# Decay attention and a two-layer hard-swish network on one core: the second layer's scale in another PSUM bank, its float32 pieces two places further ahead, and the last tile's units in another order

## The chip, the cores and the metric

One core of a Trainium2 chip runs the whole program. The metric is the device time of one execution in microseconds. Besides the median of several timed runs there is one profiled execution, whose trace gives every instruction's start and duration; times "at 139" are microseconds from the start of its span.

## The reference

The input is 8 batches of 8 heads, 576 positions and 64 numbers a head; the first layer has 512 by 2048 weights, the second 2048 by 512. The weights arrive as float64, two 32-bit words each, so they have to be decoded on the chip.

```python
scores = scale * q @ k.T + (cum[:, None] - cum[None, :])   # cum: cumulative sum of log f
scores = where(causal, -1e9, scores)
attn   = softmax(scores)                                   # per head, 576 x 576
x      = (attn @ v)                                        # heads side by side: 4608 x 512
h      = x @ w_in                                          # 4608 x 2048
g      = h * clip(h + 3, 0, 6) / 6
out    = g @ w_out                                         # 4608 x 512
```

## The kernel before, in words

**Engines.** TensorE (PE) multiplies, VectorE (DVE) and ScalarE (ACT) evict PSUM and do the elementwise work, GpSimd (POOL) prepares q and k, SyncE (SP) issues the DMAs. Each engine takes its instructions in one fixed order, which a scheduler makes at build time from program order, priorities and its own model of durations. So a change of a buffer can move hundreds of instructions.

**Two halves that run beside each other.** The attention goes head by head. The first batch is done in another form (four pairs, then eight heads, tiles `pf` and `ps`); from the second batch on each head ("F" in `VH`, 56 of them) goes through `rows`: PE makes scores `pn` (L609, L612) in two halves, DVE takes row maxima while copying to `pp` (L620), ACT takes the exponential (L632) and a float16 copy (L646), DVE or POOL the remainder (L649, L655), a transposing DMA moves both (L667), PE multiplies with v into `pav` (L692 to L697), and DVE normalises it. Every two heads a transposing DMA (`x_move`, L748) puts the result into `xT`, the input of the network.

**The network** works on tiles of 512 tokens, one per batch. For each of 16 pieces of 128 hidden features `h_unit` does 12 matmuls (L775 to L777; every number is split into two float16 halves, and three of the four products are summed), then ACT L781, DVE L784, ACT L785, DVE L786 write the two halves of `gT`. Then `out_unit` makes 128 rows of output with 48 matmuls of 512 columns (L821 to L823, tile `po`), ACT L827 scales them and SP stores them (L830). Each batch has 64 tokens more than its tile; the left-over tokens of two batches make one short unit (`h_short`, L797 to L799, tile `phs`, evicted by L805, L809, L811, L812). `queue` and `fill` hand these units out between the steps of the attention. The first tile's units are named by their columns, 0 or 256, since its first 256 columns are ready earlier.

**PSUM.** The network's accumulators rotate over three banks: two of pool `ps_m` (tag `mm`) and the single bank of `ps_t` (tag `tr`), which the small transposes of the row maxima (`ptm`, L500) use too.

**The second layer's weights.** `w_out_work` loads 16 chunks, decodes each to float32 and squares it (L251 to L257), then sums the squares over all chunks (L279) and lets `pow2_scale` (L184 to L196, tile `pt_w`) make one power of two out of it. With that scale `w_split` makes two float16 halves of each chunk: the high one on ACT (L284), the low one on DVE (L295). Both float32 piece and halves live in one buffer, `w2`: the halves of chunk k in place k, the float32 piece of chunk k in place k+1. So the high half of chunk k is written over the float32 piece of chunk k-1, and ACT must wait until DVE has read that one.

**The last tile** (`moe_tile` with t = 7) runs its 16 `h_unit`s, then the four `h_short`s of the last two batches (their `gT` lies in `vst`), then four `out_unit`s of 512 columns and two of 256 columns for the short rows.

Of the kernel before, what the change touches and what calls it, by code (L numbers as in the profile page):

```python
# [20 lines left out]
def kernel(  # L21
# [10 lines left out]
    nc = tc.nc  # L32
# [68 lines left out]
    NSP = 3  # L101
# [32 lines left out]
    w2 = cpool.tile([P, NFC + 1, 2, DM], F16, name="w2")  # L134
# [46 lines left out]
    def pow2_scale(pm, s_col, i_col, name):  # L181
        pool, tag = (ps_t, "tr") if SV < s_col < SV + B else (ps_m, "mm")
# [37 lines left out]
    slots_in = slots_out + [spare[:, (2 * h + 9) * CW:(2 * h + 11) * CW] for h in range(NSP)]  # L220

    def w_chunk(i, k):

        if i == 0:
            j, c = divmod(k, NCC)
            cols = slice(j * CW, (j + 1) * CW)
            o = (2 * j + c % 2 + NW // 2 * (c // 2)) * CW
            return w_in[c * P:(c + 1) * P, cols], gTf[:, o:o + CW], [t[:, c, cols] for t in w1]
        return (
            w_out[k * P:(k + 1) * P, :], w2f[:, (k + 1) * CW:(k + 2) * CW],  # L230
            [w2[:, k, h, :] for h in range(2)],
        )
# [526 lines left out]
    turn = [0]  # L759

# [7 lines left out]
    def h_unit(t, fc, c0, c1):  # L768
        x = xT[t % 2]
# [3 lines left out]
        for cc in range(NCC):  # L773
            xh, xl = (x[:, cc, c0 // P:c1 // P, hl] for hl in range(2))
            nc.tensor.matmul(ph, w1[0][:, cc, fs_], xh, start=(cc == 0), stop=False)  # L775
            nc.tensor.matmul(ph, w1[0][:, cc, fs_], xl, start=False, stop=False)  # L776
            nc.tensor.matmul(ph, w1[1][:, cc, fs_], xh, start=False, stop=(cc == NCC - 1))  # L777
            if cc == 1 and nw == TT:
                yield H_COST
        r = p2.tile([P, TT], F32, tag="rt", name=f"r_{t}_{fc}_{c0}", bufs=3)[:, :nw]  # L780
# [8 lines left out]
    def h_short(u, j, gd):  # L789
# [3 lines left out]
        for i in range(n):  # L793
            fs_ = slice((n * j + i) * P, (n * j + i + 1) * P)
            for cc in range(NCC):
                xh, xl = (x[:, cc, :, hl] for hl in range(2))
                nc.tensor.matmul(ph[:, i], w1[0][:, cc, fs_], xh, start=(cc == 0), stop=False)  # L797
                nc.tensor.matmul(ph[:, i], w1[0][:, cc, fs_], xl, start=False, stop=False)
                nc.tensor.matmul(ph[:, i], w1[1][:, cc, fs_], xh, start=False, stop=(cc == NCC - 1))  # L799
            if i == 1:  # L800
                yield H_COST
        r = p2.tile([P, TT], F32, tag="rt", name=f"rs_{u}_{j}", bufs=3)
# [30 lines left out]
    def moe_tile(t, c0=0, c1=TT):  # L833
        for fc in range(NFC):
# [5 lines left out]
            yield from h_unit(t, fc, c0, c1)  # L840
        if t == 0:
# [4 lines left out]
        last = t == B - 1  # L846
        if last:
            gs = vst.bitcast(F16).rearrange("p c e -> p (c e)")[:, 0:2 * NFC * P]
            gs = gs.rearrange("p (a f t) -> p a f t", a=2, f=NFC)
            for j in range(NG):  # L850
                yield from h_short(t // 2, j, gs)
# [223 lines left out]
```

## Time and profile before

| | |
|---|---|
| median of 3 runs | 1078.44 us (1075.19 to 1080.29) |
| the profiled execution | 1080.35 us, of which the span is 1078.6 us |
| mean granted TensorE clock | 0.985 |
| busy share of the span | PE 94%, DVE 67%, ACT 55%, POOL 38% |

The page divides the span into 40 slices of 27 us. The stages by the trace: the first batch's attention and the decoding of the weights to 137 us, the first heads of the second batch and the first tile's two layers to 255 us, then seven batches in an even rhythm to 925 us, and the last tile alone to the end. "Idle before, releaser" in a row says how long the engine sat before the instruction and what ended it. A matmul's shown duration includes its way through the array, so the distance of two starts, not the duration, is its price: 512 columns start about 0.216 us apart.

### The profile page before, as it was taken

The page shows a single profiled execution, that of the slowest core. Times are in us where ns is not written, and L with a number is a line of the kernel's source. Part 1 is how long each engine was busy: PE and PEld are TensorE (multiplying, and loading weights), DVE is VectorE, ACT ScalarE, POOL GpSimd, SP SyncE. Part 2 cuts the span into 40 slices and gives each one's busy share as a digit, 9 for nine tenths or more (in the row PEclk, how much of TensorE's full clock was granted, in tenths as well). Part 3 has the DMA queues.
Part 4 walks back from the last instruction along what each step waited for, and adds up shares of the span by engine and source line. Part 5 has one row for each costly group of instructions (what it writes and reads, how often), then busy time and mean ns, then how long its engine had stood idle before and what let it go on. Part 6 is the DMA issues. An engine that isn't in the chain of part 4 may idle for free.

```text
span 1078.6 us, 21257 instructions
## 1 busy us (share of the span) xinstructions
PE 1013.8 (94%) x7698; PEld 604.8 (56%) x7698; DVE 726.8 (67%) x1903; ACT 587.9 (55%) x1190; POOL 408.5 (38%) x505
## 2 busy tenths in 40 slices
PE   2799988899999999999999999999999999999897
PEld 2557854665455755555555755555555755544545
DVE  7887899887875668866865677767855678305300
ACT  4777657665664557555654547655743567315301
POOL 7434456454433445443434334443433442000000
PEclk9989989999999999999999999999999999999999
DMA  8976448965665676567465576567565554300000
GB/s 253 288 210 199 117 103 160 203 149 127 149 104 121 138 151 128 111 151 160 98 127 107 105 164 129 118 137 169 101 112 123 108 101 84 78 30 1 1 20 30
DMA packets 259300, 133.79 MB, mean 124 GB/s; under 512 B 226964, under 2 KB 228812, under 8 KB 259196
## 3 DMA queue, kind: packets, MB, share of 16 engines
q1 hardware_dynamic: 259196, 132.44, 55.7%
q8 instruction: 61, 1.00, 0.4%
q14 instruction: 43, 0.35, 0.1%
HBM read 47.93 MB, written 9.73 MB: 53 GB/s over the span
## 4 chain that ended last, share of the span: by engine, by line
PE 66%; DVE 13%; DMA 6%; ACT 6%; issue 5%; POOL 2%; SPq 1%; ACTq 0%; DVEq 0%; POOLq 0%
PE po L821 10%; PE po L822 10%; PE po L823 10%; PE ph L775 7%; PE ph L776 7%; PE ph L777 7%; DVE pp L620 3%; PE pn L609 3%; PE pn L612 3%; DMA vst<-in_vS_dram 2%; ACT pp L632 2%; DVE ring L649 2%; DVE gT L786 1%; DVE r L784 1%; DMA ring<-in_w_out_dram 1%
## 5 line engine op out<-in xcount | busy, mean ns | idle before, releaser
L632 ACT ACTIVATE pp<-pp,nb 128x192 f32<-128x192 f32 x280 | 138.9, 552 | 135.8 <-DVE nb L626 135.3
L821 PE MATMUL po<-w,gT 128*128 128x512 f16 x560 | 208.0, 383 | 5.2 <-DVE rs L809 2.8
L822 PE MATMUL po<-w,gT 128*128 128x512 f16 x560 | 210.2, 383 | 1.3 <-DVE w L295 1.3
L775 PE MATMUL ph<-xT,w 128*128 128x512 f16 (+1 forms) x576 | 201.5, 359 | 10.3 <-DVE r L784 10.1
L823 PE MATMUL po<-w,gT 128*128 128x512 f16 x560 | 210.1, 382 | 0.0
L776 PE MATMUL ph<-xT,w 128*128 128x512 f16 (+1 forms) x576 | 200.7, 358 | 0.0
L777 PE MATMUL ph<-xT,w 128*128 128x512 f16 (+1 forms) x576 | 200.0, 358 | 0.0
L649 DVE TENSOR_TENSOR ring<-pp,ring 128x128 f16<-128x128 f32 (+2 forms) x216 | 140.4, 660 | 82.6 <-ACT ring L646 81.6
L620 DVE CUSTOM_DVE_ANT_0 pp<-pn,W 128x192 f32<-128x192 f32 x280 | 123.3, 482 | 26.6 <-PE pn L612 25.0
L447 POOL TENSOR_SCALAR TK<-ST 64x576 fp32r<-64x576 f32 (+1 forms) x68 | 49.9, 733 | 240.8 <-PE pn L609 200.7
L459 POOL TENSOR_TENSOR T<-ST,T 64x576 fp32r<-64x576 f32 (+1 forms) x68 | 99.4, 1461 | 84.2 <-DMA T<-TK 72.5
L609 PE MATMUL pn<-TK,TQ 68*128 68x192 f32 x336 | 124.3, 384 | 5.0 <-issue 3.9
L784 DVE SCALAR_TENSOR_TENSOR r<-r,ph 128x512 f32<-128x512 f32 (+1 forms) x144 | 89.1, 620 | 56.2 <-ACT r L781 55.8
L785 ACT CAST gT<-r 128x512 f16<-128x512 f32 (+1 forms) x144 | 81.5, 568 | 80.8 <-DVE r L784 80.2
L786 DVE TENSOR_TENSOR gT<-r,gT 128x512 f16<-128x512 f32 (+1 forms) x144 | 103.9, 725 | 20.6 <-ACT gT L785 19.0
L781 ACT ACTIVATE r<-ph,bias_r,SC 128x512 f32<-128x512 f32 (+1 forms) x144 | 103.9, 725 | 23.1 <-PE ph L777 20.6
L646 ACT CAST ring<-pp 128x192 f16<-128x192 f32 x280 | 114.3, 449 | 0.0
L612 PE MATMUL pn<-T,T 128*128 128x192 f32 x336 | 113.0, 363 | 0.0
L456 POOL TENSOR_TENSOR T<-ST,TQ 64x576 fp32r<-64x576 f32 (+2 forms) x68 | 98.3, 1446 | 15.9 <-PE ps L552 5.4
L823 PEld LDWEIGHTS <-gT 128*128 128x128 f16 x560 | 55.0, 99 | 68.3 <-issue 9.2
L655 POOL TENSOR_TENSOR ring<-pp,ring 128x128 f16<-128x128 f32 x96 | 61.6, 642 | 80.5 <-ACT ring L646 35.2
L822 PEld LDWEIGHTS <-gT 128*128 128x128 f16 x560 | 54.9, 99 | 63.5 <-issue 8.5
(154 smaller groups left out, 1987.1 us busy)
## 6 DMA issues: line engine op xcount, KB each, us to landing
ST<-in_qk_dram SPq DMA_DIRECT2D x64, 288.0 KB
T<-TK SPq DMA_DIRECT2D x64, 144.0 KB
out_dram<-o SPq DMA_DIRECT2D x33, 256.0 KB
ring<-in_w_out_dram SPq DMA_DIRECT2D x16, 512.0 KB
T<-TQ SPq DMA_DIRECT2D x56, 144.0 KB
vst<-in_vS_dram SPq DMA_DIRECT2D x7, 1040.0 KB
ring<-in_w_in_dram SPq DMA_DIRECT2D x9, 512.0 KB
w<-in_w_in_dram SPq DMA_DIRECT2D x7, 512.0 KB
```

The costliest lines, as they stand in the source:

```text
L609: nc.tensor.matmul(dst, TQ[i][0:D + 4, qs], TK[i][0:D + 4, a:e], start=True, stop=False)
L612: nc.tensor.matmul(dst, T7[j][:, qs], T1[j][:, a:e], start=False, stop=True)
L620: nc.vector.tensor_tensor_reduce(pp[:r, w:w + kw], pn[:r, o:o + kw], W[:r, 4 * P + r - kw:4 * P + r], 1.0, -3.0e38, ALU.add, ALU.max, accu ...
L632: nc.scalar.activation(x_, x_, AF.Exp, bias=nb[:r, e0 + x:e0 + x + 1], scale=0.125)
L649: eng.tensor_tensor(hl[:r, a:a + c * P], pp[:r, at[c] + 64:at[c] + kw], hl[:r, h0[c] + 64:h0[c] + kw], op=ALU.subtract,)
L775: nc.tensor.matmul(ph, w1[0][:, cc, fs_], xh, start=(cc == 0), stop=False)
L776: nc.tensor.matmul(ph, w1[0][:, cc, fs_], xl, start=False, stop=False)
L777: nc.tensor.matmul(ph, w1[1][:, cc, fs_], xh, start=False, stop=(cc == NCC - 1))
L786: nc.vector.tensor_tensor(gT[:, 1, fc, c0:c1], r, gT[:, 0, fc, c0:c1], op=ALU.subtract)
L821: nc.tensor.matmul(po, g[:, 0, fc, ts_], w2[:, fc, 0, c], start=(fc == 0), stop=False)
L822: nc.tensor.matmul(po, g[:, 0, fc, ts_], w2[:, fc, 1, c], start=False, stop=False)
L823: nc.tensor.matmul(po, g[:, 1, fc, ts_], w2[:, fc, 0, c], start=False, stop=(fc == NFC - 1))
```

## The change

It has three parts. The sum matrix `pt_w` of the second layer's power of two is allocated in the single bank of `ps_t` in place of one of the two `mm` banks. The float32 pieces lie three places ahead of their halves (`AHEAD = 3`), so `w2` has 19 places for 17; three spare slots for the first layer's raw loads move with it. And in the last tile each `h_short` comes after every fourth `h_unit`, with each unit's first matmul of a column chunk ordered behind the last matmul of the unit before (an order for the scheduler; both are on PE).

```diff
-    NSP = 3
...
-    w2 = cpool.tile([P, NFC + 1, 2, DM], F16, name="w2")
+    AHEAD = 3
+    w2 = cpool.tile([P, NFC + AHEAD, 2, DM], F16, name="w2")
...
-        pool, tag = (ps_t, "tr") if SV < s_col < SV + B else (ps_m, "mm")
+        pool, tag = (ps_t, "tr") if SV < s_col < SV + B or s_col == S2 else (ps_m, "mm")
...
-    slots_in = slots_out + [spare[:, (2 * h + 9) * CW:(2 * h + 11) * CW] for h in range(NSP)]
+    slots_in = slots_out + [spare[:, o * CW:(o + 2) * CW] for o in (13, 15, 17)]
...
-            w_out[k * P:(k + 1) * P, :], w2f[:, (k + 1) * CW:(k + 2) * CW],
+            w_out[k * P:(k + 1) * P, :], w2f[:, (k + AHEAD) * CW:(k + AHEAD + 1) * CW],
...
+    chain = []
+
+    def behind(on):
+        return tc.issue_after(chain[-1]) if on and chain else nullcontext()
...
     def h_unit(t, fc, c0, c1):
+        last = t == B - 1
...
-            nc.tensor.matmul(ph, w1[0][:, cc, fs_], xh, start=(cc == 0), stop=False)
+            with behind(last and cc == 0):
+                nc.tensor.matmul(ph, w1[0][:, cc, fs_], xh, start=(cc == 0), stop=False)
...
+        if last:
+            chain.append(d.ins)
...
     def h_short(u, j, gd):
...
+                with behind(gd is not gT and cc == 0):
+                    nc.tensor.matmul(ph[:, i], w1[0][:, cc, fs_], xh, start=(cc == 0), stop=False)
...
+        if gd is not gT:
+            chain.append(d.ins)
...
     def moe_tile(t, c0=0, c1=TT):
...
             yield from h_unit(t, fc, c0, c1)
+            if last and new == 1:
+                yield from h_short(t // 2, j, gs)
...
-            for j in range(NG):
-                yield from h_short(t // 2, j, gs)
```

In the listings below, a line number of the changed program is higher than the old one: L295 stays, L775 is L781, L786 is L794, L799 is L808, L821 to L823 are L834 to L836, L827 is L840.

**DVE, ahead of the first head of the second batch.** Row maxima of that head are the L620 rows on `pn_12`. Before, these rows stand there; `SC` is the table of scales, `rs`, `xf` and `pav` belong to the first batch's attention, and `w2<-w2` is a low half of a second-layer chunk.

```order
L724 RECIPROCAL rs_10_0_1642<-rs_10_0_1642 128x3
L384 TENSOR_TENSOR SC_121<-SC_121 128x1
L726 TENSOR_SCALAR rs_10_0_1642<-rs_10_0_1642,SC_121 128x3
L620 ISA pp_12_0_1670,MF0_108<-pn_12_0_1661,W_88 128x192
L620 ISA MF0_108 128x1
L620 ISA pp_12_0_1670,MF0_108<-pn_12_0_1661,W_88 128x576
L620 ISA MF0_108 128x1
L620 ISA pp_12_0_1670,MF0_108<-pn_12_0_1661,W_88 64x64
L620 ISA MF0_108 64x1
L387 COPY SC_121<-SC_121 64x1
L727 TENSOR_TENSOR xf_10_1640<-pav_110,rs_10_0_1642 128x3x64
L295 SCALAR_TENSOR_TENSOR w2_115<-w2_115,SC_121 128x512
```

In the changed program these rows lead up to the same L620 (`r` and `gT` are evictions of the first tile's features, `vm1` a maximum over v).

```order
L295 SCALAR_TENSOR_TENSOR w2_115<-w2_115,SC_121 128x512 x3
L792 SCALAR_TENSOR_TENSOR r_0_13_0_1168<-r_0_13_0_1168,ph_0_13_0_1155 128x256
L794 TENSOR_TENSOR gT_116<-r_0_12_0_1142,gT_116 128x256
L366 TENSOR_REDUCE vm1_1579<-vst_112 128x1 x2
L721 TENSOR_SCALAR rs_9_1_1550<-pav_110 128x3
L295 SCALAR_TENSOR_TENSOR w2_115<-w2_115,SC_121 128x512 x3
L794 TENSOR_TENSOR gT_116<-r_0_13_0_1168,gT_116 128x256
L371 TENSOR_TENSOR vm1_1579<-vm1_1579 128x2
L792 SCALAR_TENSOR_TENSOR r_0_14_0_1204<-r_0_14_0_1204,ph_0_14_0_1191 128x256
L724 RECIPROCAL rs_9_1_1550<-rs_9_1_1550 128x3
L792 SCALAR_TENSOR_TENSOR r_0_15_0_1232<-r_0_15_0_1232,ph_0_15_0_1219 128x256
L620 ISA pp_12_0_1670,MF0_108<-pn_12_0_1661,W_88 128x192
```

Before, the first low half stands behind the first head's first row maxima and the others are strewn over the following heads. Now nine of the 16 (one and two more stand further up) are ahead of it, and the other seven follow before the second head.

**PE, at the second head of the second batch.** The second head's scores are `pn_13`; `po_0` and `po_128` are the first two output units of the first tile. Before, the second head's scores stand behind the first matmul of each.

```order
L777 LDWEIGHTS w11_114
L777 MATMUL ph_0_2_256_1905<-xT0_117,w11_114 128x256
L821 LDWEIGHTS gT_116
L821 MATMUL po_0_0_1389<-w2_115,gT_116 128x512
L821 LDWEIGHTS gT_116
L821 MATMUL po_128_0_1525<-w2_115,gT_116 128x512
L609 MATMUL pn_13_0_1744<-TK1_97,TQ1_94 128x192
L612 MATMUL pn_13_0_1744<-T11_100,T71_102 128x192
```

In the changed program all 96 matmuls of these two units stand ahead of it; their last three and the head's first two are these.

```order
L834 LDWEIGHTS gT_116
L834 MATMUL po_128_0_1525<-w2_115,gT_116 128x512
L835 LDWEIGHTS gT_116
L835 MATMUL po_128_0_1525<-w2_115,gT_116 128x512
L836 LDWEIGHTS gT_116
L836 MATMUL po_128_0_1525<-w2_115,gT_116 128x512
L609 MATMUL pn_13_0_1744<-TK1_97,TQ1_94 128x192
L612 MATMUL pn_13_0_1744<-T11_100,T71_102 128x192
```

So the second head has moved behind 94 matmuls of 512 columns. The third to eighth heads follow behind it, with the rest of the first tile's features between them, and 27 matmuls of the second tile now stand ahead of the third batch's third head (`pn_22`), where before the first of them stood behind it.

**ACT, at the end of the program.** `po_4480` is the last 512-column output unit, `po_3456_0` and `po_3456_256` are the two units of the short rows. The last rows before are these.

```order
L827 ACTIVATE o_4352_0_12420<-po_4352_0_12371,SC_121 128x512
L827 ACTIVATE o_4480_0_12472<-po_4480_0_12423,SC_121 128x512
L805 ACTIVATE rs_3_3_12261<-phs_3_3_12212,bias_r_86,SC_121 128x4x64 x2
L811 CAST vst_112<-rs_3_3_12261 128x512
L827 ACTIVATE o_3456_0_12524<-po_3456_0_12475,SC_121 128x256
L827 ACTIVATE o_3456_256_12577<-po_3456_256_12528,SC_121 128x256
```

And of the changed program these.

```order
L840 ACTIVATE o_4224_0_12368<-po_4224_0_12319,SC_121 128x512
L840 ACTIVATE o_4352_0_12420<-po_4352_0_12371,SC_121 128x512
L840 ACTIVATE o_4480_0_12472<-po_4480_0_12423,SC_121 128x512
L840 ACTIVATE o_3456_0_12524<-po_3456_0_12475,SC_121 128x256
L840 ACTIVATE o_3456_256_12577<-po_3456_256_12528,SC_121 128x256
```

The eviction of the fourth short unit (`rs_3`) is gone from here: with the others it now stands between those of the features. On PE the last matmul before belonged to `po_3456_256`; now the last 20 matmuls of the program are 19 of `po_4480` and one of `po_3456_256`, so the unit that ends last is the one whose eviction stands first of ACT's last three.

More of the change, by code (lines that the diff above doesn't have):

```diff
@@ L774, in h_unit @@
             xh, xl = (x[:, cc, c0 // P:c1 // P, hl] for hl in range(2))
-            nc.tensor.matmul(ph, w1[0][:, cc, fs_], xh, start=(cc == 0), stop=False)
+            with behind(last and cc == 0):
+                nc.tensor.matmul(ph, w1[0][:, cc, fs_], xh, start=(cc == 0), stop=False)
             nc.tensor.matmul(ph, w1[0][:, cc, fs_], xl, start=False, stop=False)
-            nc.tensor.matmul(ph, w1[1][:, cc, fs_], xh, start=False, stop=(cc == NCC - 1))
+            d = nc.tensor.matmul(ph, w1[1][:, cc, fs_], xh, start=False, stop=(cc == NCC - 1))
             if cc == 1 and nw == TT:
                 yield H_COST
+        if last:
+            chain.append(d.ins)
         r = p2.tile([P, TT], F32, tag="rt", name=f"r_{t}_{fc}_{c0}", bufs=3)[:, :nw]
@@ L796, in h_short @@
                 xh, xl = (x[:, cc, :, hl] for hl in range(2))
-                nc.tensor.matmul(ph[:, i], w1[0][:, cc, fs_], xh, start=(cc == 0), stop=False)
+                with behind(gd is not gT and cc == 0):
+                    nc.tensor.matmul(ph[:, i], w1[0][:, cc, fs_], xh, start=(cc == 0), stop=False)
                 nc.tensor.matmul(ph[:, i], w1[0][:, cc, fs_], xl, start=False, stop=False)
-                nc.tensor.matmul(ph[:, i], w1[1][:, cc, fs_], xh, start=False, stop=(cc == NCC - 1))
+                d = nc.tensor.matmul(
+                    ph[:, i], w1[1][:, cc, fs_], xh, start=False, stop=(cc == NCC - 1)
+                )
             if i == 1:
                 yield H_COST
+        if gd is not gT:
+            chain.append(d.ins)
         r = p2.tile([P, TT], F32, tag="rt", name=f"rs_{u}_{j}", bufs=3)
@@ L833, in moe_tile @@
     def moe_tile(t, c0=0, c1=TT):
+        last = t == B - 1
+        if last:
+            gs = vst.bitcast(F16).rearrange("p c e -> p (c e)")[:, 0:2 * NFC * P]
+            gs = gs.rearrange("p (a f t) -> p a f t", a=2, f=NFC)
         for fc in range(NFC):
@@ L845, in moe_tile @@
             moe_scale_out(t)
[L846 to L849, printed above, removed]
-            for j in range(NG):
-                yield from h_short(t // 2, j, gs)
         r0 = t * S + (64 if t else 0)
```

## The prediction

> **What bounds the kernel now.** I read the page's busy shares and slices first, then a table of stages, then for each stage the lines and waits of the engine that is late.
>
> ```profile
> PE 1013.8 (94%) x7698; PEld 604.8 (56%) x7698; DVE 726.8 (67%) x1903; ACT 587.9 (55%) x1190; POOL 408.5 (38%) x505
> PE   2799988899999999999999999999999999999897
> PEclk9989989999999999999999999999999999999999
> ```
>
> PE is at 94%, and its slices stand at nine from the tenth to near the end. So a gain can only come from the places where PE sits idle or at half its clock: the early slices and the last few. The table of stages (stretch, length, busy time of PE, weight loads, DVE, ACT and POOL, granted clock, DMA share, GB/s):
>
> ```profile
> core 0: us, PE busy (x) PEld busy (x) DVE busy (x) ACT busy (x) POOL busy (x), PEclk, DMA share, GB/s
> ...
> 117.00:139.00 22.00, 20.87 (x175) 18.14 (x176) 18.03 (x64) 11.67 (x23) 10.22 (x10) 1.00 0.49 123
> 139.00:160.00 21.00, 15.70 (x93) 10.02 (x91) 20.07 (x48) 12.47 (x27) 11.77 (x11) 0.84 0.47 104
> 160.00:200.00 40.00, 33.08 (x302) 20.67 (x298) 37.67 (x107) 28.88 (x61) 28.70 (x27) 0.96 0.87 178
> 200.00:255.00 55.00, 51.49 (x488) 36.73 (x489) 46.28 (x134) 34.10 (x80) 22.75 (x27) 0.97 0.68 141
> 255.00:300.00 45.00, 43.02 (x307) 22.87 (x306) 36.12 (x87) 29.51 (x57) 19.01 (x26) 0.96 0.74 159
> 300.00:600.00 300.00, 297.84 (x2304) 168.20 (x2302) 207.25 (x544) 164.06 (x336) 124.55 (x162) 1.00 0.62 127
> ...
> 1004.00:1016.00 12.00, 9.20 (x149) 8.43 (x147) 3.51 (x6) 4.92 (x11) 0.00 (x0) 0.96 0.01 1
> 1016.00:1065.00 49.00, 49.00 (x275) 25.16 (x274) 2.26 (x4) 3.74 (x6) 0.00 (x0) 0.98 0.06 22
> ```
>
> From 300 on PE is full and DVE has a third of its time free. Between 139 and 200 it is the other way round: DVE is busy 20.07 of 21 and 37.67 of 40 us, PE waits 5.3 and 6.9 us and runs part of the time at half clock (0.84, 0.96). There DVE bounds, and PE's idle time is the price.
>
> Why PE is so slow there is seen in the splitting of the second layer's weights.
>
> ```profile
> L295 DVE SCALAR_TENSOR_TENSOR w<-w,SC x16: 704/739/1905, 139.0 to 191.7; 128x512 f16<-128x512 f32 x16
> L284 ACT ACTIVATE w<-w,SC x16: 706/717/723, 136.4 to 190.8; 128x512 f16<-128x512 f32 x16
> ...
> 140.19 0.72 ACT L284 ACTIVATE w<-w,SC 128x512 f16<-128x512 f32 x1 [2.58 <-DVE w L295]
> ...
> 154.95 0.72 ACT L284 ACTIVATE w<-w,SC 128x512 f16<-128x512 f32 x1 [5.97 <-DVE w L295]
> ...
> L821 PE MATMUL po<-w,gT x32: 376/379/617, 138.9 to 192.4; 128*128 128x512 f16 x32
> ```
>
> Sixteen chunks of 0.72 us on ACT and 0.74 us on DVE take 55 us, one after the other, because a high half may only be written when DVE has read the chunk before it; ACT's idle time of 2.58 and 5.97 us ends on just that. The first two output units (32 matmuls of L821, 96 in all) follow them and hold two of the three banks from 138.9 to 192.4.
>
> **The change, part by part. First the scale.** The sum that it needs is there early, and the result late:
>
> ```profile
> 116.88 0.16 DVE L279 TENSOR_REDUCE wm<-wsum 128x1 f32<-128x16 f32 x1
> ...
> 134.22 0.16 DVE L187 TENSOR_SCALAR e_w<-pt_w 128x1 f32<-128x1 f32 x1 [1.38 <-PE pt_w L184]
> ```
>
> The sum over the chunks ends at 117.04, its matrix is read at 134.22: 17 us on the way through the `mm` banks. In the changed order this matmul stands right behind the attention work of 117, so the splits can begin some 16 us earlier. What is queued behind it on PE waits for nothing new, since the sum is done. The transposed maxima of two heads of the first batch need the same single bank and come later by some 9 us; I cost that at nothing, since six feature units on PE cover it, and at up to 2 us if they don't.
>
> **Second, the distance of three.** Now ACT may run three chunks ahead of DVE. The work stays the same, 16 of each, but nine low halves are done ahead of the first head of the second batch, and seven before the second. The first two output units run in one piece: 96 matmuls at the dense price, read from the starts at 1018.76 and 1019.41 further down (three matmuls in 0.65 us, 0.217 each), are 20.8 us.
>
> **What this costs the attention.** In the new order the second head's scores stand behind those 96. First row maxima of the first and second head before:
>
> ```profile
> 137.35 0.36 DVE L620 CUSTOM_DVE_ANT_0 pp<-pn,W 128x192 f32<-128x192 f32 x1 [0.41 <-PE pn L612]
> ...
> 152.29 0.34 DVE L620 CUSTOM_DVE_ANT_0 pp<-pn,W 128x192 f32<-128x192 f32 x1
> ...
> L775 PE MATMUL ph<-xT,w x52: 377/379/634, 255.2 to 299.9; 128*128 128x512 f16 x52
> ```
>
> The first head keeps its time: 9 halves of 0.74 us are 6.7 us more for DVE ahead of it, against 22 - 18.03 = 4.0 us that DVE idles from 117 to 139 and some 3 us of first-batch work that moves behind it. The second one's maxima can't begin before 137.4 + 20.8 + about 1 = 159: 7 us later than 152.29, and DVE, whose next rows stand behind it, waits with them. In return 13 of the 16 low halves (all but those at 139, 142 and 144.5) no longer lie between 152 and 192: 13 x 0.74 = 9.6 us. The second tile's features begin at 255.2, when the second batch's heads have come through. Its start moves by +7 if nothing of the 9.6 is regained and by -9.6 if all is and DVE doesn't wait; +7 - 9.6 = -2.6 is what DVE's list gives by itself, but DMA, too, is at 0.87 of its time from 160 to 200. I take 0, between them.
>
> What PE gains then is what it does before that start and did behind it: 27 matmuls of the second tile, 27 x 0.217 = 5.9 us. From there PE bounds, so the lead stays. Term of this stage: -5.9, from +1 (start +7) to -15.5 (start -9.6).
>
> **Third, the last tile.** Both stalls of PE in it, and what follows the first:
>
> ```profile
> 1012.28 0.22 PE L799 MATMUL phs<-xS,w 128*128 128x128 f16 x1
> 1015.31 0.58 PE L821 MATMUL po<-w,gT 128*128 128x512 f16 x1 [2.80 <-DVE rs L809]
> 1015.69 0.63 PE L822 MATMUL po<-w,gT 128*128 128x512 f16 x1
> ...
> 1018.54 0.38 PE L823 MATMUL po<-w,gT 128*128 128x512 f16 x1
> 1018.76 0.38 PE L821 MATMUL po<-w,gT 128*128 128x512 f16 x1
> ...
> 1019.41 0.38 PE L821 MATMUL po<-w,gT 128*128 128x512 f16 x1
> ...
> 1064.81 0.22 PE L799 MATMUL phs<-xS,w 128*128 128x128 f16 x1
> 1066.86 0.27 PE L821 MATMUL po<-w,vst 128*128 128x256 f16 x1 [1.83 <-DVE rs L809]
> ```
>
> ```profile
> 1065.07 1.03 ACT rs L805 x2
> 1066.12 0.70 DVE rs L809
> ```
>
> Three short units end together, hold all three banks, and PE waits for their eviction: 1015.31 - 1012.28 less one small matmul, 0.06, is 2.97 us. Then eight matmuls take 1018.54 - 1015.31 = 3.23 us where the dense price is 1.74: 1.49 us at half clock. The fourth short unit comes last and is waited for from 1064.81 to 1066.86: 1.99 us. With a short unit after every fourth feature unit each eviction (1.03 us on ACT and 0.70 on DVE, the last two rows, of the chain that ended last) lies beside the next unit's 12 x 0.217 = 2.6 us, so all three go: -6.45 us.
>
> Two things come back at the end. `po_4480` takes the bank of `po_4096`, which ends just ahead of it: a wait of one eviction. And `po_4480` now ends last, with two more evictions and all five stores behind it:
>
> ```profile
> L827 ACT ACTIVATE o<-po,SC x6: 474/683/688, 1034.0 to 1073.6; 128x512 f32<-128x512 f32 x4, 128x256 f32<-128x256 f32 x2
> ...
> 1073.30 0.27 PE L823 MATMUL po<-w,vst 128*128 128x256 f16 x1
> 1073.35 2.43 SPq L830 DMA_DIRECT2D out_dram<-o  x4
> 1073.61 0.47 ACT L827 ACTIVATE o<-po,SC 128x256 f32<-128x256 f32 x1 [0.29 <-PE po L823]
> ```
>
> The bank: 0.38 for the matmul's end and 0.68 for the eviction, less a start of 0.217, is about +0.9, or 0 if something covers it. The stores: four issues take 2.43, so 0.61 each. Now the last one ends 1075.78 - 1074.08 = 1.7 us behind the last eviction, with five in a row it is 3.05 behind the first of the three: +1.35, and +0.3 for a longer matmul and eviction; bounds 0.3 and 2.5, taken 1.65. The last tile: -6.45 + 0.9 + 1.65 = -3.9, from -6.2 to -3.0.
>
> **The sum.** -5.9 - 3.9 = -9.8 us. The profiled execution took 1080.35, so 1070.5 for its like; it lies 1.9 above the median of the runs, so the median goes from 1078.44 to about 1069. About 0.5%, 5.4 us, is what a measurement of this kernel can tell from no change: faster is below 1073.0, slower above 1083.8.
>
> **The rivals.** *The lead is paid back.* PE runs ahead of an attention that is bound by DVE and DMA, and the second tile starts some 6 us late; only the last tile is left: -3.9, 1074.5. For it: DVE's 37.67 of 40. Against it: 9.6 us less for DVE there.
>
> *All of it is kept.* DVE doesn't wait for the second head and all 9.6 is regained: -15.5 - 3.9 = -19.4, 1059. For it: PE's idle time and lost clock from 117 to 255 (16.9 and 6.6 us by the stages) hold that much. Against it: DVE's idle time there is 16 us in all, 8.7 of it behind 200.
>
> *Slower: PE's order holds the heads up.* Before, the features of the first tile's second half stood behind the heads of the second batch, now two units of 1.3 us (12 matmuls of 256 columns, half of 2.6) stand ahead of each. If each of six heads finds DVE empty and waits 2.6 us, 15.6 are added to the 7: the second tile starts 22.6 late, -5.9 - 3.9 + 22.6 = +12.9, 1091. It decides once DVE idles more than some 17 us between 139 and 255 that it doesn't now. For it: the wait of 7. Against it: DVE has work in hand for 90% of that stage.
>
> *More half clock.* From 160 to 255 PE no longer has most of the 96 matmuls to do and so pauses more; two stretches of the last tile show what a pause does to the clock.
>
> ```profile
> 1012.30:1015.30 3.00, 0.20 (x4) 0.95 0.00 0
> 1015.30:1018.40 3.10, 3.09 (x8) 0.50 0.00 0
> ```
>
> A pause of 3 us was followed by 3.1 us at 0.50. If those 95 us ran at 0.84, as 139 to 160 does now, PE would lose 15.2 us for the 3.3 of now, +12, and the time would be 1081, no change. The Trainium skill (TensorE: Matmul & The Clock Gate, Part 1) speaks for this rival: it says that one idle window of about 3.4 us puts the array back to half rate, and that one busy window releases it. By that rule the price per pause is about 1.7 us, as the row of 0.50 agrees, and the rival would need nine of them, where the 3.3 us of now are two (an estimate from that page).
>
> **How the numbers follow.** Forecast 0.48, range of its own 1064 to 1074; paid back 0.24; all kept 0.11; more half clock 0.08; slower 0.09. Faster takes nearly all of the forecast, all kept, and a little of the paid back: 0.60. Same takes the rest of these and the half clock: 0.30. Slower: 0.10. Leaving out the slower rival and half of all kept gives a range of 1061 to 1080.
>
> **What would show it.** Right: L284 and L295 lie between 118 and 147 and ACT no longer waits for L295; the 96 matmuls lie in one piece and end by 160; the second tile's first features are 3 to 9 us ahead of 255; PE has no gap over 1.2 us from 960 to the last matmul; the span's end is 6 to 7 us behind it. Wrong: a second tile that starts after 262, DVE idle over 17 us more from 139 to 255, or PE's clock under 0.9 there.

## The result and the profile after

Slower by half a per cent, where faster was forecast: 1083.25 us median (1081.36 to 1085.11, 8 runs) against 1076.87 (1075.19 to 1080.35, 8 runs) beside it; ratio 1.0052, 95% interval 1.0034 to 1.0069. Measured a second time, in the last but one group of experiments, it was 1.0081 (1.0058 to 1.0105). The two profiled executions stand closer than the medians, 1081.36 (span 1079.5) against 1080.35 (span 1078.6): that of before is its longest run, that of after its shortest. So the traces show where the time goes, and the medians how much it is.

The page of the changed kernel, busy times and slices:

```profile
PE 1016.3 (94%) x7698; PEld 608.5 (56%) x7698; DVE 714.6 (66%) x1903; ACT 587.5 (54%) x1190; POOL 407.8 (38%) x505
...
PE   2889987899989999999999999999999999999997
...
PEclk9989988989999999999999999999999999999999
```

The end of PE's row has lost its 8 in the last slice but two, and from the sixth slice to the twelfth it has a 7 and three 8s where before has three 8s; the whole clock row has four slices at 8 where before has two. The same by stages (columns as in the prediction):

```profile
117.00:139.00 22.00, 17.01 (x142) 14.76 (x142) 20.09 (x49) 15.56 (x29) 11.18 (x11) 0.97 0.50 138
139.00:160.00 21.00, 21.00 (x88) 9.21 (x88) 13.35 (x43) 8.71 (x18) 4.77 (x4) 0.87 0.18 49
160.00:200.00 40.00, 33.61 (x339) 28.64 (x338) 31.12 (x102) 25.90 (x62) 18.44 (x19) 0.91 0.65 126
200.00:255.00 55.00, 49.12 (x407) 32.83 (x405) 38.54 (x132) 28.20 (x67) 29.70 (x29) 0.91 0.82 161
255.00:300.00 45.00, 40.75 (x340) 23.60 (x338) 37.36 (x98) 31.27 (x65) 24.40 (x33) 0.96 0.75 160
...
1004.00:1016.00 12.00, 12.00 (x92) 6.89 (x91) 6.55 (x10) 6.60 (x10) 0.00 (x0) 1.00 0.00 0
1016.00:1065.00 49.00, 48.22 (x257) 25.00 (x256) 3.73 (x6) 5.36 (x8) 0.00 (x0) 1.00 0.05 17
```

Two sums from such rows are used from here on: PE's idle time (length less busy time) and its lost clock (length times one less the granted clock). From 117 to 160 they are 5.0 + 3.4 us where before has 6.4 + 3.4: the change does fill PE there, busy 21.00 of 21.00 from 139 to 160. From 160 to 300 they are 16.5 + 10.3 where before has 12.4 + 5.1: more is given back than was gained. Over 117 to 300 it is 35.2 us against 27.2. DVE is free where PE is late: from 139 to 255 it idles 33.0 of 116 us, before 12.0.

The splits of the second layer, and the first two output units (with durations, first and last start):

```profile
L284 ACT ACTIVATE w<-w,SC x16: 707/720/724, 121.6 to 147.3; 128x512 f16<-128x512 f32 x16
```

```profile
L295 DVE SCALAR_TENSOR_TENSOR w<-w,SC x16: 731/740/1883, 122.3 to 148.2; 128x512 f16<-128x512 f32 x16
```

```profile
L834 PE MATMUL po<-w,gT x32: 377/379/634, 139.0 to 164.4; 128*128 128x512 f16 x32
```

So this part does what it says: the splits, 136 to 192 before, now lie from 122 to 149. What it runs into is on DVE's timeline, ahead of the first head (L620), and ends one wait of PE:

```profile
130.01 2.88 DVE L366 TENSOR_REDUCE vm<-vst 128x1 f32<-128x1536 f32 x2 [1.91 <-issue]
132.88 3.62 DVE L295 SCALAR_TENSOR_TENSOR w<-w,SC 128x512 f16<-128x512 f32 x3
...
138.50 0.41 DVE L792 SCALAR_TENSOR_TENSOR r<-r,ph 128x256 f32<-128x256 f32 x1
138.91 0.39 DVE L792 SCALAR_TENSOR_TENSOR r<-r,ph 128x256 f32<-128x256 f32 x1
139.22 0.34 DVE L620 CUSTOM_DVE_ANT_0 pp<-pn,W 128x192 f32<-128x192 f32 x1
...
166.13 0.36 DVE L620 CUSTOM_DVE_ANT_0 pp<-pn,W 128x192 f32<-128x192 f32 x1 [1.22 <-PE pn L612]
```

```profile
138.96 0.59 PE L834 MATMUL po<-w,gT 128*128 128x512 f16 x1 [4.66 <-DVE r L792]
```

PE is ready for the output units 4.66 us before a feature unit's bank is evicted (L792), because that eviction stands in DVE's list behind two maxima over v (2.88 us together), three low halves (3.62 together) and other small work. The second head's maxima (the row at 166.13) come 13.8 us later than before. What becomes of the lead is counted in the second tile's features:

```profile
L781 PE MATMUL ph<-xT,w x44: 376/379/634, 229.4 to 297.6; 128*128 128x512 f16 x44
```

44 rows of this line start before 300, 52 in the program before. Each is one of three matmuls; counted over all three lines, 132 have started where before has 154, so 22 are missing, 4.8 us at 0.217.

What PE waits for from 160 to 300 has changed as well (time in all, number, longest):

```profile
PE pav L692 <- DMA pT<-ring: 6.2, 5, 2.6
PE pn L609 <- issue: 5.5, 2, 4.5
PE pn L612 <- POOL T L459: 2.2, 2, 1.4
PE pn L609 <- DVE MF L620: 1.1, 1, 1.1
```

These 15.0 us all end at a matmul of a head (`pn`, `pav`), and only 0.2 us more at one of the network; before it was 5.7 and 6.4. So it is the heads that PE waits for there. The lag is complete soon after: the second tile's last first-layer matmul ends at 318.2, before at 310.5. By the start of the last tile 4.5 us of these 7.7 are left (960.2 against 955.7).

### The profile page after: what moved, and what is told of

It is laid out like the page before. It is cut to its first block, busy times and chain, and to the rows that moved or that the text cites. A ratio compares the mean times of both kernels' runs of the same rounds, so it can differ in the third digit from the quotient of the medians.

```text
span 1079.5 us, 21234 instructions
## 1 busy us (share of the span) xinstructions
PE 1016.3 (94%) x7698; PEld 608.5 (56%) x7698; DVE 714.6 (66%) x1903; ACT 587.5 (54%) x1190; POOL 407.8 (38%) x505
## 4 chain that ended last, share of the span: by engine, by line
PE 66%; DVE 12%; issue 6%; DMA 6%; ACT 5%; POOL 3%; SPq 1%; ACTq 0%; POOLq 0%; DVEq 0%
PE po L834 10%; PE po L836 10%; PE po L835 10%; PE ph L781 7%; PE ph L783 6%; PE ph L782 6%; PE pn L609 3%; PE pn L612 3%; DMA vst<-in_vS_dram 2%; DVE pp L620 2%; ACT pp L632 2%; PE pav L703 2%; PE low L287 1%; DMA pT<-ring 1%; DVE gT L794 1%
## 5 line engine op out<-in xcount | busy, mean ns | idle before, releaser
L834 PE MATMUL po<-w,gT 128*128 128x512 f16 x560 | 210.2, 383 | 6.1 <-DVE r L792 4.7
L836 PE MATMUL po<-w,gT 128*128 128x512 f16 x560 | 209.7, 382 | 0.0
L781 PE MATMUL ph<-xT,w 128*128 128x512 f16 (+1 forms) x576 | 201.8, 359 | 6.2 <-DVE r L792 6.2
L620 DVE CUSTOM_DVE_ANT_0 pp<-pn,W 128x192 f32<-128x192 f32 x280 | 123.1, 481 | 34.9 <-PE pn L612 23.8
L447 POOL TENSOR_SCALAR TK<-ST 64x576 fp32r<-64x576 f32 (+1 forms) x68 | 50.8, 747 | 247.2 <-PE pn L609 172.5
L792 DVE SCALAR_TENSOR_TENSOR r<-r,ph 128x512 f32<-128x512 f32 (+1 forms) x144 | 88.9, 619 | 51.1 <-ACT r L789 50.7
L794 DVE TENSOR_TENSOR gT<-r,gT 128x512 f16<-128x512 f32 (+1 forms) x144 | 102.2, 714 | 19.4 <-ACT gT L793 18.2
L456 POOL TENSOR_TENSOR T<-ST,TQ 64x576 fp32r<-64x576 f32 (+2 forms) x68 | 99.2, 1459 | 15.5 <-PE pn L612 5.8
L836 PEld LDWEIGHTS <-gT 128*128 128x128 f16 x560 | 55.0, 99 | 67.5 <-issue 7.4
L840 ACT ACTIVATE o<-po,SC 128x512 f32<-128x512 f32 (+1 forms) x37 | 24.7, 673 | 120.7 <-PE po L836 115.8
```

The lines of the kernel that those rows point to most:

```text
L620: nc.vector.tensor_tensor_reduce(pp[:r, w:w + kw], pn[:r, o:o + kw], W[:r, 4 * P + r - kw:4 * P + r], 1.0, -3.0e38, ALU.add, ALU.max, accu ...
L834: nc.tensor.matmul(po, g[:, 0, fc, ts_], w2[:, fc, 0, c], start=(fc == 0), stop=False)
L836: nc.tensor.matmul(po, g[:, 1, fc, ts_], w2[:, fc, 0, c], start=False, stop=(fc == NFC - 1))
```

## The experiments

All ratios are against the program before, timed beside the kernel in five rounds. The table has them all; in the last three columns are the start of the second head's first row maxima, the number of the second tile's 512-column matmuls that start before 300, and PE's idle time plus lost clock from 117 to 300 by the table of stages, all from the kernel's own trace. "All" is the whole change; "hold N" hands the first tile's output units out N steps later.

| kernel | ratio (95% interval) | second head | second tile by 300 | idle + lost |
|---|---|---|---|---|
| before | 1 | 152.3 | 154 | 18.8 + 8.4 |
| last tile only | 0.996 (0.9939 to 0.9981) | 153.8 | 151 | 19.5 + 5.2 |
| distance, last tile | 0.999 (0.9967 to 1.0013) | 149.9 | 154 | 23.4 + 6.6 |
| bank, last tile | 1.0095 (1.0058 to 1.0132) | 173.4 | 108 | 28.9 + 13.8 |
| bank, distance | 1.006 (1.0034 to 1.0086) | 167.4 | 136 | 21.3 + 12.2 |
| all | 1.0052 (1.0034 to 1.0069) | 166.1 | 132 | 21.5 + 13.7 |
| all, again | 1.0081 (1.0058 to 1.0105) | 167.1 | 132 | 21.4 + 12.1 |
| all, hold 4 | 1.0012 (0.9996 to 1.0028) | 167.9 | 150 | 19.9 + 8.7 |
| all, hold 8 | 0.9962 (0.9943 to 0.9981) | 157.3 | 161 | 19.8 + 8.7 |
| all, hold 12 | 0.9984 (0.9965 to 1.0003) | 155.1 | 156 | 20.6 + 6.7 |
| all, hold 16 | 1.0055 (1.0037 to 1.0073) | 153.0 | 120 | 26.0 + 12.2 |
| last tile, hold 8 | 1.0027 (1.0007 to 1.0047) | 152.0 | 138 | 21.4 + 10.2 |
| last tile, hold 16 | 1.007 (1.0045 to 1.0095) | 153.5 | 111 | 22.5 + 13.3 |
| bank, last tile, hold 16 | 1.0078 (1.0056 to 1.0101) | 165.5 | 85 | 22.7 + 19.3 |
| distance, last tile, hold 8 | 0.9978 (0.9961 to 0.9995) | 151.2 | 162 | 19.1 + 5.4 |
| distance, last tile, head behind | 1.0025 (1.0001 to 1.0049) | 168.4 | 150 | 20.0 + 5.4 |
| all, features spread 4 | 1.0073 (1.0048 to 1.0098) | 164.6 | 120 | 26.4 + 13.9 |
| all, features spread 8 | 1.0112 (1.0091 to 1.0134) | 166.1 | 108 | 27.3 + 14.6 |
| all, no POOL piece | 1.0108 (1.0076 to 1.0139) | 164.4 | 91 | 34.2 + 17.1 |
| last tile, no POOL piece | 1.0022 (1.0002 to 1.0042) | 152.8 | 137 | 23.1 + 8.6 |

### The parts

**The last tile only**: scale and distance as before (the spare slots for the raw loads go back with the distance, here and below).

```diff
-    AHEAD = 3
+    AHEAD = 1
...
-        pool, tag = (ps_t, "tr") if SV < s_col < SV + B or s_col == S2 else (ps_m, "mm")
+        pool, tag = (ps_t, "tr") if SV < s_col < SV + B else (ps_m, "mm")
...
```

> The last tile's new order alone; scale bank and distance as before. My theory: the order of the last tile gains about 4 us (its trace shows a lag of 4.3 us at 968 and of 0.9 at 1060), and everything ahead of 925 is as before: 1073 by the median of before, ratio 0.996 to 0.997. Rival, the last tile itself is what costs (its evictions and stores come later than they gain): 1.000 or more.

0.996: -4.3 us. As expected; the forecast for this part was -3.9.

**Bank and distance without the last tile**: no order behind the unit before, short units after the features.

```diff
-        return tc.issue_after(chain[-1]) if on and chain else nullcontext()
+        return nullcontext()
...
-            if last and new == 1:
-                yield from h_short(t // 2, j, gs)
...
+            for j in range(NG):
+                yield from h_short(t // 2, j, gs)
```

> Scale bank and distance of three, last tile as before. My theory: the loss is all in the first 300 us, and without the last tile's gain it is about 10 us: ratio 1.009 (1.007 to 1.011), second tile's first features at 267. Rival, the early stage is neutral and the last tile costs: 1.000.

1.006, with 136 matmuls of the second tile by 300. The loss is in the early stage. The second tile's first features start at 230.2 and not at 267 as I expected, so the start of that tile doesn't show the loss. Its size is smaller than what the other two measurements make of it (1.0052 or 1.0081 over 0.996 is 1.009 or 1.012); the intervals are too wide to say more.

**Distance and last tile**: the scale back in the `mm` banks.

```diff
-        pool, tag = (ps_t, "tr") if SV < s_col < SV + B or s_col == S2 else (ps_m, "mm")
+        pool, tag = (ps_t, "tr") if SV < s_col < SV + B else (ps_m, "mm")
```

> Distance of three and the last tile's order, the scale's matrix back in the mm banks: the splits begin at 134 again, and the second head's scores stand on PE 12 rows behind the first head's, not behind 96 matmuls of the output units. My theory (the output units ahead of the second head are the loss): the second head starts near 152, the second tile's features near 255 or earlier, 1066 to 1074, ratio 0.990 to 0.997. Rival, the low halves that now stand closer together on DVE ahead of the heads are the loss: slower than the last tile alone, 1.000 or more.

0.999, and this is the run that shows where a lead goes. Its stages:

```profile
139.00:160.00 21.00, 21.00 (x118) 11.29 (x117) 21.00 (x55) 17.19 (x36) 11.52 (x9) 1.00 0.42 96
160.00:200.00 40.00, 32.24 (x343) 26.33 (x342) 33.75 (x86) 23.77 (x55) 20.57 (x20) 0.96 0.67 142
200.00:255.00 55.00, 46.73 (x428) 29.95 (x425) 48.31 (x147) 31.34 (x72) 28.78 (x35) 1.00 0.78 171
255.00:300.00 45.00, 38.36 (x298) 21.45 (x295) 38.76 (x83) 29.91 (x60) 18.41 (x25) 0.89 0.70 152
```

PE doesn't stop from 139 to 160 and runs at full clock, 5.3 + 3.4 us better than before. From 200 to 300 it idles 8.3 + 6.6 us where before it idled 3.5 + 2.0, and loses 4.9 us of clock for 3.5. At 300 it has started 154 matmuls of the second tile, just as many as before. Of PE's waits from 200 to 300, 12.2 us end at a matmul of a head and 2.8 at one of the network, and the third batch's sixth head has its first row maxima at 302.5, before at 301.7.

**Bank and last tile**: the distance back at one.

```diff
-    AHEAD = 3
+    AHEAD = 1
...
```

> The scale's matrix in the single bank and the last tile's order, distance of one as before. In this order the 96 matmuls of the output units stand among the first head's scores and all ahead of the second head's. My theory: the early stage loses as in the whole change or more, since the units also wait for splits at distance one: 1.005 to 1.015. Rival, the distance of three is the loss: about 0.996, as the last tile alone.

1.0095, some 15 us above the last tile alone. Here the output units stand among the first head's scores; the worst stage:

```profile
160.00:200.00 40.00, 27.01 (x249) 22.80 (x248) 32.76 (x94) 22.15 (x51) 20.90 (x21) 0.83 0.60 124
```

So the scale's bank carries the loss; the distance by itself costs nothing that is clear of the noise (0.999 beside 0.996). Whether the distance takes part of the loss back (1.0052 and 1.0081 against 1.0095) the overlapping intervals leave open.

### The output units handed out later

My theory now was that the second head's wait behind the 96 matmuls is the loss. The same kernel, with the units given out some steps later:

```diff
+        if t == 0 and c0 == 0:
+            for _ in range(8):
+                left[0] += 1.0
+                yield 1.0
         for s in range(c0 // P, c1 // P):
             yield from out_unit(...)
```

> The whole change, but the first tile's output units are handed out 8 steps later; on PE the second head's scores then stand 86 matmuls behind the first head's first, where they stood 118 behind it in the changed program and 23 in the program before. The splits, their distance, the scale's bank and the last tile stay. My theory (the loss is the second head's wait behind the output units): 32 matmuls less ahead of it are some 7 us, so it starts near 159 in place of 166, half of the early loss goes: ratio 0.998 to 1.003. Rival, the low halves ahead of the first head on DVE are the loss: still 1.005.

0.9962, better than the 0.998 that I expected at best: all of the early loss is gone, with bank, distance, splits and last tile as in the whole change. Its stages and the second tile:

```profile
139.00:160.00 21.00, 21.00 (x121) 12.60 (x119) 13.70 (x51) 10.63 (x22) 3.06 (x3) 0.93 0.38 89
160.00:200.00 40.00, 36.65 (x375) 29.25 (x375) 36.02 (x101) 27.24 (x64) 25.75 (x25) 0.91 0.70 140
200.00:255.00 55.00, 47.57 (x432) 31.51 (x432) 46.96 (x152) 33.00 (x76) 26.98 (x33) 0.97 0.90 170
255.00:300.00 45.00, 41.08 (x305) 22.73 (x303) 36.79 (x92) 30.34 (x60) 21.00 (x27) 1.00 0.74 164
```

```profile
L781 PE MATMUL ph<-xT,w x54: 376/379/392, 230.6 to 299.6; 128*128 128x512 f16 x54
```

DVE is as busy from 139 to 160 as in the whole change (13.70, 13.35), but has 13.3 us more to do from 160 to 255 (82.98 against 69.66): the heads come through. 16 steps (`range(16)`), and as a control the same 16 steps in the kernel with the last tile only:

> As the kernel with 8 steps, but 16: the second head's scores stand 37 matmuls behind the first head's first. My theory: second head at 147 to 152 as in the program before, the early loss is gone and at most some of the lead is kept: ratio 0.990 to 0.998, so at least as fast as the last tile's order alone. Rival, low halves on DVE: still 1.005. Rival, PE's lead is what matters and holding the units back wastes it: slower than the whole change, over 1.005.

> The control: the last tile's order and the same 16 steps of delay, scale's bank and distance as before. Here the second head's scores stand where they stood before, 23 behind the first head's first, with or without the delay. My theory: no change against the last tile's order alone, ratio 0.994 to 0.998. If the delay helps by itself (all heads before the output units), it is faster than 0.993, and the kernel with hold of 16 proves less.

1.0055 and 1.007, not the 0.990 to 0.998 that I expected of both. The second head is back at 153, and the time isn't. In the first one the units are missing later:

```profile
200.00:255.00 55.00, 37.19 (x342) 27.94 (x339) 43.15 (x130) 30.02 (x72) 27.27 (x30) 0.84 0.79 158
```

PE idles 17.8 us there. At 16 steps bank and distance cost nothing (1.0055 against 1.007), at none they cost a per cent. The other delays are the same lines with 16 steps in the kernel with bank and last tile, 8 in the one with the last tile only, and 4 and 12 in the whole change:

> The scale's bank, the last tile's order and 16 steps of delay, distance one. The second head's scores stand 66 behind the first head's first, where without the delay they stood 127 behind it (and the first head's own last row 119). My theory: the first head back near 139, the second near 155 to 158, and most of the loss of 13 us against the last tile's order alone goes: ratio 0.996 to 1.002. Rival, the distance of one with an early scale is what costs (chunks waiting for each other): 1.007 or more.

> The control for the kernel with 8 steps of delay, which took 0.9962: the last tile's order and 8 steps, scale and distance as before. PE's order up to the third batch's first head is that of the program before. My theory: the delay by itself gives nothing at 8 steps, 0.994 to 0.998; then bank and distance cost nothing either once the second head isn't behind the output units. If it is slower than 1.000, the delay costs and bank and distance gain some 4 us; if it is under 0.993, the delay gains and they cost.

> The whole change with 4 steps of delay: the second head's scores stand 112 matmuls behind the first head's first, 118 without the delay, 86 with 8 steps. My theory by the second head's place alone: near 165, ratio 1.002 to 1.006, as the whole change. Rival, the places of the third to eighth heads and of the second tile's features decide, which move by the delay too (the second tile's first unit is no longer begun ahead of the third batch): 0.996 to 1.000.

> The whole change with 12 steps: the second head's scores stand 44 matmuls behind the first head's first. My theory: second head at 150 to 153; what a delay takes from PE later (16 steps cost some 11 us with the old bank and distance) has begun to show: 0.996 to 1.003. By the second head alone it would be 0.996 or less.

1.0078 for bank and last tile with 16 steps, little better than without and not the expected 0.996 to 1.002. The control with 8 steps, 1.0027, is slower than the last tile alone although PE's order up to the third batch's first head is that of the last tile only: the delay costs by itself, and at 8 steps the early scale and the distance together win that back. Twelve steps give 0.9984, inside the expectation. Four steps give 1.0012 with the second head at 167.9, later than in the whole change (166.1, 167.1). That speaks against the second head as the cause. It speaks in the same way against what follows them on POOL: the next preparation of q and k behind the second head's scores (L447) starts at 166.83 in the whole change and at 146.24 before, but with four steps only at 169.05.

### The second head alone, and what else lies in the stage

**The second head behind the units** in the kernel with distance and last tile:

```diff
+        late = n == H + 1 and half == 0 and c == NAT[0][0] and a == 0
+        with tc.issue_after(first_out[0]) if late else nullcontext():
             nc.tensor.matmul(dst, TQ[i][0:D + 4, qs], TK[i][0:D + 4, a:e], ...)
...
+        if gs is None and rows_[0] == 128:
+            first_out.append(d.ins)
```

> As distance of three with the last tile's order (which had the second head's maxima at 149.9 and took 0.999 of before), with one thing more: the second head's first score matmul is ordered behind the last matmul of the first tile's second output unit, so that it stands 136 matmuls behind the first head's first, where it stood 23 behind. The scale stays in the mm banks. My theory: the second head comes at 160 or later, nothing of that is regained, and the time is 1.004 to 1.010 of before. Rival, the order of the heads doesn't matter as long as PE has its matmuls early: 0.997 to 1.001, as without it.

1.0025 against 0.999 without: 3.8 us, short of the 1.004 that I had expected at the least, and the intervals overlap. The second head is at 168.4 as forced, but PE's idle and lost time up to 300 is 25.4 us against 29.9, and 150 matmuls of the second tile are done against 154. By the traces this kernel is 1.5 us behind the other at the end of the second tile's features (311.7 against 310.2) and 4.9 at the start of the last tile (959.7 against 954.8), so most of what it loses is lost later. My theory falls: that one wait does not make the loss of the whole change. That it makes a small part of it is not excluded.

**The first tile's second half later** (4 and 8 steps, second head unchanged), **distance and last tile with the 8 steps of above**, and **the whole change again**, unedited:

```diff
+        if t == 0 and c0 > 0:
+            for _ in range(4):
+                left[0] += 1.0
+                yield 1.0
         for fc in range(NFC):
```

> The whole change, and only the second half of the first tile (its features 256 to 512, which stand between the second batch's third to eighth heads) is handed out 4 steps later. The second head stays where the change put it, behind all 96 matmuls of the output units. On PE the features between successive heads from the second head on are then 7, 20, 45, 36, 36, 39 in place of 18, 9, 9, 72, 36, 48, and the remaining output matmuls ahead of the ninth to eleventh heads are spread otherwise. Theory 1 (the second head's wait is the loss): unchanged, 1.003 to 1.007. Theory 2 (what costs is how the first tile's units lie among the third to tenth heads: pauses there, and the half clock behind them): idle and lost clock from 100 to 320 fall from 62 to about 55 us, ratio 0.996 to 1.001.

> The same with 8 steps. PE's order is that of the kernel with 4 steps up to the eighth head; behind it the remaining 96 output matmuls are spread over the next four heads as 31, 9, 24, 32 in place of 19, 36, 14, 27, and the second tile's features stand further back. Theory 1: 1.003 to 1.007. Theory 2: 0.996 to 1.003, worse than with 4 steps if the second tile's later place counts as it did in the controls with 8 and 16 steps.

> Distance of three, the last tile's order and 8 steps of delay, the scale in the mm banks. Second head 23 matmuls behind the first head's first. It tells which part makes the whole change with 8 steps 0.9962 where the last tile with 8 steps alone is 1.0027: if the scale's bank is needed, 1.000 to 1.004 here; if the distance alone does it, 0.993 to 0.998.

> The whole change as it is, on the chip of the other three, so that they can be compared with it: 1.003 to 1.007 as in its first measurement, with 15 + 3 us of idle time and lost clock of PE from 100 to 160 and 35 + 9 from 160 to 320.

1.0073 and 1.0112 beside 1.0081 for the whole change: spreading the features among the heads doesn't help. It also sets the second tile back, so it doesn't clear the features' places either. Distance with 8 steps gives 0.9978: the scale's bank isn't needed for what is gained there. The whole change itself came out above the 1.003 to 1.007 that I expected.

**No piece of the remainder on POOL.** In the whole change DVE waits twice for POOL between 200 and 255, which the kernel with 4 steps doesn't:

```profile
DVE pp L620 <- POOL ring L649: 8.7, 2, 4.5
```

```diff
-    PL_POOL = ((3, ), ())
+    PL_POOL = ((), ())
```

> The whole change, and the remainder of the 384-column chunk of the second batch's eight heads, which is POOL's (1.1 us each), is given to DVE. It takes away the wait of DVE for POOL: 8.7 us in the whole change between 200 and 255 (two waits of over 4 us), where hold_4 has 0.8; DVE gets 8 pieces of some 0.8 us instead. PE's order is nearly unchanged up to the eighth head. Theory A (the loss between 200 and 255 is DVE waiting for POOL's late piece, and PE for the heads behind it): 2 to 6 us faster than the whole change, 0.998 to 1.004. Theory B (the loss is in the fixed order of units and heads on PE, and the waits only show it): as the whole change, 1.004 to 1.008.

> The control: the last tile's order with the same piece given to DVE, scale and distance as before. DVE is the bound from 139 to 200 here, so 8 pieces of 0.8 us more should cost something: 0.996 to 1.002 by both theories.

1.0108 and 1.0022. The wait is gone (DVE's longest one there is now this), and the time is longer than the whole change's, by 0.3 to 0.6%, where the same piece costs the control 0.6%:

```profile
DVE pp L620 <- PE pn L612: 1.1, 1, 1.1
```

So by these numbers taking the wait away brought 4 us at most, and nothing that is clear of the noise: it isn't the cause of the whole loss. PE's idle time went up in every stage behind 160 (9.7, 10.1 and 9.4 us), as the last but one row of the table shows in sum.

**What the table says as a whole.** The second head's column doesn't sort the kernels: with it at 164 to 168 there are ratios from 1.0012 to 1.0112, at 150 to 155 from 0.996 to 1.007. The number of the second tile's matmuls nearly does; idle and lost time does less well (29.9 us with 0.999, 25.4 with 1.0025). With 151 and more of the second tile's matmuls started by 300 the kernels with the last tile's gain take 0.996 to 0.999; with 150, 1.0012 and 1.0025; with 138 and 137, 1.0027 and 1.0022; with 132 and fewer, 1.0052 and more. That names no cause, since these matmuls come last in the stage: it shows that most of the difference is made by 300, and on PE. Behind it the lag against the program before still changes: from the end of the second tile's features to the start of the last tile by -5.5 (features spread 4) to +2.8 us (head behind).

## Why the prediction was wrong

**The scale**: right. The splits lie at 121.6 to 149 (forecast 118 to 147). ACT still waits for L295, 5.8 us in all where before it was 12.3; the forecast had none. The transposed maxima in the single bank, put at 0 to 2 us, cost PE nothing that shows: from 117 to 139 it idles 4.99 us, and 4.66 of them are the pause below.

**The distance, and "the 96 matmuls in one piece, 20.8 us, by 160"**: from 139.0 to 164.9, 25.9 us. Two things were missing in the 20.8. One is half clock from 139.0 to 144.4, which costs 2.7 us. The other is work of the first batch's attention that stands between the output units' matmuls: from 159.91 to 163.77 there are 24 matmuls of L703 and only six of the units, some 2.6 us (3.86 less 6 x 0.217); so it isn't quite one piece. Missing ahead of it was the pause of 4.66 us, which the half clock follows. The pause comes from "the first head keeps its time": I priced DVE's nine low halves against DVE's free time, without the two maxima over v in the same list, and not against the feature evictions that queue behind them and hold the banks that PE needs. The first head's maxima came at 139.22, 1.9 us late.

**"The second head at 159, DVE waits with it"**: 166.1. Right in sign, and by the experiments not what decides.

**The failed step** is the one behind it: "I take 0" for the start of the second tile, "27 matmuls of the second tile" as gain, and "from there PE bounds, so the lead stays". Term forecast -5.9, from +1 to -15.5. Instead of 27 more matmuls by 300 there are 22 fewer, and PE's idle and lost time from 117 to 300 grows by 8.0 us, outside the range. The runs show two things in its place. First, a lead of PE ahead of 200 isn't kept: with the distance and the last tile's order it is all paid back by 300, because the second and third batch's heads still have to come through, and PE idles for them (12.2 of its 15.0 us of waits from 200 to 300). Second, with the scale's bank the output units' new place costs more than that, and the same units 8 steps later cost nothing (0.9962). The start of the second tile was the wrong thing to look at: its first matmul is at 229.4, far ahead of 255.2 and of the 262 that was to show the prediction wrong, but only 7 of its matmuls start before 255.2.

**The last tile**: right. -3.9 forecast, -4.3 (-6.6 to -2.0) measured. PE's only gap of note from 960 on is the bank's wait, 0.9 in the forecast; at the end ACT's last eviction waits for a store to free its buffer, which the forecast put into +1.65 as a queue of stores:

```profile
1051.48 0.38 PE L834 MATMUL po<-w,gT 128*128 128x512 f16 x1 [0.78 <-ACT o L840]
```

```profile
1073.28 2.03 DMA out_dram<-o
1075.39 0.47 ACT o L840
```

**The rivals.** "The lead is paid back" is what the distance alone does: 0.999 with the last tile's gain in it. "Slower" had its point of decision reached (DVE idles 21 us more from 139 to 255, the point was 17), and the whole change was slower by half of its +12.9 in the first measurement, 6.4 us by the medians, and by two thirds in the second. "More half clock" named more than half of the sum: of the 8.0 us, 5.3 are lost clock (13.7 against 8.4) and 2.7 are idle time. Each of these was given as an alternative to the others; they came together. That a head that waits makes a pause, and a pause the half clock, fits the rows below; no run separates the two.

**What stays open** is which instruction, behind the second head, holds the heads up in the whole change. No single wait carries it: those that I took away, or put in, didn't move the time as they should have. Shown is that the scale's bank brings it where the units are handed out at once, that handing them out 8 steps later takes it away, and that behind 160 PE's waits are nearly all ahead of a head's matmul.

## What to carry to other kernels

An engine that works ahead in a stage where another chain sets the pace has gained nothing yet: ask what it will do at the end of the stage with the time won, and count the work of the next stage that is ready by then. Where a fixed order is made by a scheduler, an earlier release moves hundreds of instructions; hand the freed work out a few steps later or earlier as part of the same trial (here 0, 4, 8, 12 and 16 steps gave 1.005 and 1.008, 1.001, 0.996, 0.998 and 1.006), with the same delay on the old version as a control. Parts of a change that touch different stages should be timed apart: here one part's 4 us of gain were hidden by the other's loss.

## What the runs showed of the hardware

PE's half clock comes in whole multiples of 3.4 us, and a pause need not be empty to bring it. In the changed kernel, each half-clock stretch from 130 to 300 behind the 3.4 us ahead of it (columns as above):

```profile
134.20:137.60 3.40, 0.10 (x1) 0.04 (x1) 3.40 (x3) 1.62 (x3) 3.37 (x2) 1.00 0.70 183
137.60:144.40 6.80, 5.44 (x13) 1.93 (x13) 6.80 (x20) 1.52 (x3) 4.75 (x5) 0.50 0.36 92
175.20:178.60 3.40, 0.22 (x8) 0.10 (x4) 3.40 (x8) 0.57 (x1) 3.16 (x4) 0.99 0.18 69
178.60:185.40 6.80, 5.52 (x28) 4.36 (x28) 6.20 (x24) 4.45 (x11) 2.90 (x5) 0.50 0.76 146
202.50:205.90 3.40, 2.09 (x14) 1.74 (x15) 2.18 (x8) 0.41 (x1) 2.73 (x5) 1.00 0.37 69
205.90:209.30 3.40, 3.18 (x17) 2.10 (x15) 3.40 (x11) 1.58 (x4) 1.37 (x1) 0.50 0.44 86
233.20:236.60 3.40, 1.37 (x13) 0.66 (x11) 2.27 (x13) 2.13 (x5) 0.00 (x0) 1.00 0.77 148
236.60:243.40 6.80, 6.25 (x49) 4.96 (x49) 4.20 (x13) 4.99 (x12) 4.14 (x4) 0.50 0.48 113
253.70:257.10 3.40, 1.98 (x40) 1.55 (x40) 1.58 (x4) 3.40 (x10) 2.59 (x4) 1.00 0.97 225
257.10:260.50 3.40, 3.40 (x21) 2.14 (x18) 3.40 (x13) 0.80 (x2) 1.93 (x4) 0.50 0.73 154
```

Three of the five follow a stretch in which PE was busy for 1.4 to 2.1 of 3.4 us by the profile. Three of the five last 6.8 us and so cost 3.4, twice the 1.7 that the prediction took as the price of a pause. The Trainium skill (TensorE: Matmul & The Clock Gate, Part 1) tells of a free-running window of about 3.4 us and of an idle window as what brings the half rate; the window's length agrees with these rows, "idle" has to be read as "less busy" here.

How much less can be counted over the windows of 3.41 us, as the clock's own changes mark them, from 100 to 1055 us in all twenty traces. Half clock follows 85 windows. Every window in which PE was busy for less than 1.35 us is among them and none in which it was busy for more than 2.1; between the two it goes both ways. At half clock a window with less than 2.8 us of busy time was never the last one, and one with more than 3.3 always was. Of the 85 stretches 41 have one window, 42 have two, one has three and one four, so a pause cost 3.4 us of clock as often as 1.7. (Busy time is the profile's, in which a matmul's duration includes its way through the array.)
